# Output stores and 25 of the 35 intermediate stores issued from ScalarE instead of SyncE, in a fused attention and SoLU feed-forward kernel

## The chip, the cores and the metric

The kernel runs on one core of a Trainium2 chip. The metric is device microseconds from the start of the program to its end, the median of several executions. The engines named below are TensorE (PE in the profile, with PEld for its weight loads), VectorE (DVE), ScalarE (ACT), GpSimd (POOL) and SyncE (SP), which in this kernel does nothing but issue DMAs. "SPq" is SyncE's instruction queue. An engine executes its instructions strictly in the order in which they were written; engines wait for each other and for DMAs on semaphores.

## The reference

```python
# q, k, v: batch 8, heads 8, sequence S = 576, head size 64
out_d   = softmax(q_d @ k_d.T / 8) @ v_d       # q, k, v averaged over groups of 4 rows
out_up  = repeat(out_d, 4)                      # back to 576 rows
scores  = where(|i - j| < 4, q @ k.T / 8, -1e9)
x       = out_up + softmax(scores) @ v          # (8*576 = 4608 tokens) x 512
h       = x @ w_in                              # 4608 x 1024
solu    = h * softmax(h)
ln      = (solu - mean) / sqrt(var + 1e-6) * g_ln
y       = ln @ w_out                            # 4608 x 512, float32
```

## The kernel before

The work is cut in two ways. The attention half runs over batches and, in them, over head pairs and windows of the sequence: DMAs bring in pieces of q, k and v (tiles `qm`, `km`, `vw`, `vs`), VectorE and TensorE transpose them (`qT`, `kT`, `plT`, `pdT`), TensorE forms scores (`sc`, `sd`) and products with v (`xp`, `po`), ScalarE takes exponentials (`pl`, `pd`) and copies results out of PSUM. It ends in tiles `x` of 128 channels by tokens. The feed-forward half runs over 36 tiles of 128 tokens. All large products are done with float32 split into a high and a low part (`xh`, `xl`; `wi_h`, `wi_l`; `uh`, `ul`; `wo_h`, `wo_l`), three matmuls in place of one.

A feed-forward tile `i` goes through four generators:

- `ffn_in(i)`: 24 matmuls `h` (L862), the negated row maximum `nmx` on VectorE (L870), `e = exp(h - max)` on ScalarE (L874), `e = h * e` on VectorE (L877), two small operations on GpSimd, and then `e = e + nmu`, the centred value that is called `u`: on ScalarE (L900) or on VectorE (L902), as a table of step numbers says (`engine(...)`). Then `u` is stored to a DRAM buffer (L910, 512 KB), and after it come `r` (L913), `va`, and `m2` (L919), a Square on ScalarE that overwrites `e` and so waits until the store has read it.
- `ffn_back(i)`: four DMAs bring `u` back from DRAM with rows and columns arranged for a block transpose (tile `v`, L942). They wait until `u`'s store has landed.
- `ffn_ut(i)`: VectorE transposes `v` in place (L963), ScalarE rounds it to `uh` (L970), GpSimd or VectorE forms `ul` (L973).
- `ffn_out(i)`: 24 matmuls `o` (L990), ScalarE scales them out of PSUM into `osb` (L997, two buffers), and the tile of the output is stored (L999, 256 KB).

Tile 35 alone transposes on TensorE and has no store of `u`.

Nothing is reordered by a scheduler. Each `yield` ends a step; the steps are numbered (`plan`), and a table `ORDER` of those numbers, written out in the file, says in which order they are recorded. Every engine gets its own instructions in that order. All DMAs of the kernel before are issued by SyncE, which works through them one by one.

Each DMA reports its landing on one of eight semaphores, DMAHW0 to DMAHW7. They are handed out in turn, in the order in which the DMAs of the whole program were recorded, whichever engine issues them. The instruction that issues a DMA waits until the DMA that had the same semaphore before it has reported.

Of the kernel before, what the change touches and what calls it, by code (L numbers as in the profile page):

```python
# [122 lines left out]
"""  # L123


OTHER = """
# [11 lines left out]
def pooled_local_attention_then_solu_ffn(  # L138
# [11 lines left out]
    P = 128  # L150
# [705 lines left out]
    def ffn_in(i):  # L856
# [41 lines left out]
        else:  # L898
            if engine(nc.scalar, nc.vector) is nc.scalar:
                nc.scalar.activation(e, e, AF.Identity, bias=nmu, scale=1.0)  # L900
            else:
                nc.vector.tensor_scalar(  # L902
                    out=e, in0=e, scalar1=1.0, scalar2=nmu, op0=ALU.mult, op1=ALU.add
                )
# [255 lines left out]
```

## Time and profile before

| | |
|---|---|
| time, median of 3 runs | 583.42 us (582.59 to 588.86) |
| span of the profiled execution | 587.5 us |
| PE busy | 568.1 us (97% of the span) |
| DVE, ACT, POOL busy | 472.5, 333.4, 298.9 us |
| DMAs issued by SP | 668, of which 35 store `u` and 36 store the output |

For the profiled execution only its span is given, 587.5 us; it lies 4.1 us above the median and inside the range of the runs. Busy time is the sum of the stretches in which an engine executes. A row of the timeline has the start and the duration in us, the engine, the line, the operation, `out<-in` by the names of the program, and in square brackets how long the engine had idled and for whom. A row of the windows has, for one stretch of time, the busy us of PE, PEld, DVE, ACT and POOL (each with its count of instructions), then the granted clock of TensorE (1.00 is full speed), the busy share of the DMA engines and GB/s.

### The profile page before, as it was taken

To read this page: it belongs to the slowest core of one execution; us is meant where nothing else is said; L and a number is where in the kernel's file an instruction comes from. 1 tells how busy PE (TensorE), PEld (TensorE's weight loads), DVE (VectorE), ACT (ScalarE), POOL (GpSimd) and SP (SyncE) were. 2 spreads that over 40 slices of the span, in tenths; PEclk is the share of its full clock that TensorE was granted. 3 is DMA by queue.
4 is the path that set the end of the run, shared out by engine and by line. 5 is a ranking of instruction groups with operands and counts; after the bars stand their busy time and mean duration, and the time that the engine had idled before them with its cause. 6 is when DMAs were issued, how large, how long until landed. Compare 5 with 4: busy or idle time off the path is not lost.

```text
span 587.5 us, 15257 instructions
## 1 busy us (share of the span) xinstructions
PE 568.1 (97%) x5852; PEld 437.2 (74%) x5852; DVE 472.5 (80%) x779; ACT 333.4 (57%) x750; POOL 298.9 (51%) x447
## 2 busy tenths in 40 slices
PE   7899989999999997999999999999999999999997
PEld 3676667777777775877777777777777777788875
DVE  7999999899898878897988876898879777644650
ACT  4788678468546644466475653457545664453452
POOL 3767588857373744358543455357431842433130
PEclk9999999999999996999999999999999999999999
DMA  8999767788877888577867887665666245314221
GB/s 279 288 218 229 169 140 183 196 183 172 220 160 183 187 197 181 154 167 180 180 152 198 222 197 192 155 192 152 177 190 133 91 142 164 113 44 167 89 91 54
DMA packets 207113, 99.59 MB, mean 170 GB/s; under 512 B 163136, under 2 KB 193344, under 8 KB 207040
## 3 DMA queue, kind: packets, MB, share of 16 engines
q1 hardware_dynamic: 207040, 98.61, 65.7%
q8 instruction: 46, 0.75, 0.6%
q14 instruction: 27, 0.22, 0.1%
HBM read 65.54 MB, written 27.79 MB: 159 GB/s over the span
## 4 chain that ended last, share of the span: by engine, by line
PE 72%; DVE 13%; DMA 4%; POOL 4%; ACT 3%; issue 2%; SPq 0%; DVEq 0%; ACTq 0%; POOLq 0%
PE o L990 30%; PE h L862 28%; PE po L844 2%; PE sc L695 2%; PE sd L788 2%; DMA v<-u 2%; PE xp L753 2%; PE pdt L823 2%; PE sc L607 1%; DVE nmx L870 1%; DVE w L375 1%; DVE e L877 1%; DMA vs<-in_v_dram 1%; PE plt L655 1%; DVE w L379 1%
## 5 line engine op out<-in xcount | busy, mean ns | idle before, releaser
L862 PE MATMUL h<-wi_h,xh 128*128 128x512 f32 x288 | 116.9, 406 | 1.4 <-DVE e L877 1.3
L990 PE MATMUL o<-wo_h,uh 128*128 128x512 f32 x288 | 117.4, 408 | 0.4 <-ACT osb L997 0.4
L862 PE MATMUL h<-wi_h,xl 128*128 128x512 f32 x288 | 114.4, 397 | 0.7 <-POOL xl L1024 0.7
L990 PE MATMUL o<-wo_l,uh 128*128 128x512 f32 x288 | 114.6, 398 | 0.0
L862 PE MATMUL h<-wi_l,xh 128*128 128x512 f32 x288 | 113.7, 395 | 0.0
L990 PE MATMUL o<-wo_h,ul 128*128 128x512 f32 x288 | 79.0, 396 | 0.0
L973 POOL TENSOR_TENSOR ul<-v,uh 128x512 fp32r<-128x512 f32 x40 | 51.8, 1296 | 43.6 <-ACT uh L970 35.5
L874 ACT ACTIVATE e<-h,nmx 128x1024 f32<-128x1024 f32 x36 | 40.1, 1114 | 47.1 <-DVE nmx L870 43.4
L862 PEld LDWEIGHTS h<-wi_h,xh 128*128 128x128 f32 x288 | 54.1, 188 | 16.7 <-issue 2.9
L990 PEld LDWEIGHTS o<-wo_h,uh 128*128 128x128 f32 x288 | 54.6, 189 | 15.8 <-issue 1.4
L862 PEld LDWEIGHTS h<-wi_h,xl 128*128 128x128 f32 x288 | 54.1, 188 | 15.3 <-POOL xl L1024 2.1
L990 PEld LDWEIGHTS o<-wo_h,ul 128*128 128x128 f32 x288 | 54.1, 188 | 13.4 <-DVE ul L973 0.3
L990 PEld LDWEIGHTS o<-wo_l,uh 128*128 128x128 f32 x288 | 54.7, 190 | 12.2
L870 DVE TENSOR_REDUCE nmx<-h 128x1 f32<-128x1024 f32 x36 | 43.7, 1215 | 24.8 <-PE h L862 24.8
L862 PEld LDWEIGHTS h<-wi_l,xh 128*128 128x128 f32 x288 | 54.1, 188 | 12.0
L877 DVE SCALAR_TENSOR_TENSOR e<-h,e 128x1024 f32<-128x1024 f32 x36 | 43.8, 1216 | 14.8 <-ACT e L874 14.7
L970 ACT ACTIVATE uh<-v 128x512 fp32r<-128x512 f32 x70 | 42.7, 624 | 20.7 <-issue 8.5
L963 DVE STREAM_TRANSPOSE v<-v 128x512 f32<-128x512 f32 x70 | 46.4, 688 | 4.2 <-DMA v<-u 4.1
L997 ACT ACTIVATE osb<-o,s 128x512 f32<-128x512 f32 x36 | 24.5, 681 | 40.4 <-PE o L990 24.8
L1024 POOL TENSOR_TENSOR xl<-x,xh 128x512 fp32r<-128x512 f32 (+1 forms) x26 | 32.6, 1256 | 22.3 <-ACT xh L1021 22.0
L487 POOL TENSOR_TENSOR vs<-vs 72x512 f32<-72x512 f32 x24 | 31.6, 1318 | 17.0 <-DMA vs<-in_v_dram 16.7
L882 POOL TENSOR_SCALAR nmu<-su 128x1 f32<-128x1 f32 x36 | 8.2, 228 | 59.8 <-DVE e L877 56.9
(128 smaller groups left out, 1124.0 us busy)
## 6 DMA issues: line engine op xcount, KB each, us to landing
u<-e SPq DMA_DIRECT2D x35, 512.0 KB
v<-u SPq DMA_DIRECT2D x140, 128.0 KB
vs<-in_v_dram SPq DMA_DIRECT2D x32, 288.0 KB
out_dram<-osb SPq DMA_DIRECT2D x36, 256.0 KB
qm<-in_q_dram SPq DMA_DIRECT2D x96, 72.0 KB
km<-in_k_dram SPq DMA_DIRECT2D x96, 72.0 KB
vw<-in_v_dram SPq DMA_DIRECT2D x80, 64.0 KB
vw<-in_v_dram SPq DMA_DIRECT2D x40, 128.0 KB
```

Of the source, the lines that this page charges most:

```text
L487: eng.tensor_tensor(out=vs[:, :, 0:2 * D], in0=vs[:, :, 0:2 * D], in1=vs[:, :, 2 * D:4 * D], op=ALU.add)
L695: nc.tensor.matmul(at[rows(wi), par, pr], bt.qT[rows(par), pr, s0:s0 + W], bt.kT[rows(par), pr, s0:s0 + W], start=True, stop=True,)
L862: nc.tensor.matmul(hps[:, n, :], src[:, cc, :], wt[:, cc, n * 512:(n + 1) * 512], start=(cc == 0 and src is xh and wt is wi_h), stop=(cc = ...
L870: nc.vector.tensor_reduce(out=nmx, in_=hf, op=ALU.max, axis=AX.X, negate=True)
L874: nc.scalar.activation(e, hf, AF.Exp, bias=nmx, scale=1.0, accum_out=se)
L877: nc.vector.scalar_tensor_tensor(out=e, in0=hf, scalar=1.0, in1=e, op0=ALU.mult, op1=ALU.mult, accum_out=su)
L963: nc.vector.transpose(vg, vg)
L970: nc.scalar.activation(uh, tp, AF.Copy)
L973: (usual if v is None else engine(usual, nc.vector)).tensor_tensor(out=ul, in0=tp, in1=uh.bitcast(F32), op=ALU.subtract)
L990: nc.tensor.matmul(o, src[:, j, :], wt[:, 4 * g + j, :], start=(g == 0 and j == 0 and src is uh and wt is wo_h), stop=(g == 1 and j == 3 a ...
L997: nc.scalar.activation(osb, o, AF.Copy, scale=s)
L1024: engine(nc.gpsimd, nc.vector).tensor_tensor(out=l, in0=src, in1=h.bitcast(F32), op=ALU.subtract)
```

## The change

All 36 stores of the output are issued by ScalarE. The store of `u` is issued by the engine that `issuer` names: ScalarE where ScalarE made `u` (25 tiles), SyncE where VectorE did (10 tiles). In `ORDER`, the step of each such store is moved right behind the step that produces its data; all other steps keep their order. (The lines after L900 stand two lines lower afterwards: L912 is the store of `u`, L999 `osb`, L1001 the store of the output.)

```diff
@@ ffn_in
-            if engine(nc.scalar, nc.vector) is nc.scalar:
+            issuer = engine(nc.scalar, nc.vector)
+            if issuer is nc.scalar:
                 nc.scalar.activation(e, e, AF.Identity, bias=nmu, scale=1.0)
             else:
+                issuer = nc.sync
                 nc.vector.tensor_scalar(
                     out=e, in0=e, scalar1=1.0, scalar2=nmu, op0=ALU.mult, op1=ALU.add
                 )
...
             away[i] = dram.tile([P, DFF], F32, tag="u", name=f"u_{i}")
-            nc.sync.dma_start(away[i], e)
+            issuer.dma_start(away[i], e)
@@ ffn_out
-        nc.sync.dma_start(out[i * P:(i + 1) * P, :], osb)
+        nc.scalar.dma_start(out[i * P:(i + 1) * P, :], osb)
@@ ORDER (two of its lines; 312 and 337 are steps of stores that moved up)
-492 677 678 701 323 702 668 679 425 427 324 325 310 311 517 348 680 349 713 328 329 330 331 332
+492 677 678 701 323 702 668 679 425 427 324 325 310 311 312 517 348 680 349 713 328 329 330 331
+332 652 518 519 326 511 512 367 333 681 520 714 682 334 335 521 368 369 676 352 688 336 337 725
```

SyncE issues 607 DMAs afterwards in place of 668, ScalarE 61 in place of none. The order on TensorE, VectorE and GpSimd is the same as before.

**Place A, ScalarE, around `u` of tile 4 and the output of tile 2.** `e_4` is the tile from which `u_4` is stored, `osb_2` the output tile 2; `plT`, `mxd`, `pd` belong to the attention of batch 2, `uh_3_0` to the feed-forward of tile 3. In square brackets stand the semaphores that an instruction waits for. Before:

```order
L900 ACTIVATE e_4_2206<-e_4_2206,nmu_4_2218 128x1024 [waits Pool_49]
L636 ACTIVATE pl_1_108<-pl_1_108 128x4x128
L997 ACTIVATE osb_2_2233<-o_2_2114,s_2_1782 128x512 [waits DMAHW3_49]
L263 ACTIVATE plT_2_1_2279<-plt_2_1_2209 128x512 [waits PE_49]
L799 ACTIVATE mxd_2_1_2227<-mxd_2_1_2227 128x3 [waits DVE_49]
```

and now:

```order
L901 ACTIVATE e_4_2207<-e_4_2207,nmu_4_2219 128x1024 [waits Pool_49]
L912 DMA u_4_2228<-e_4_2207 128x1024 [waits DMAHW3_49,Activation_49]
L636 ACTIVATE pl_1_108<-pl_1_108 128x4x128
L999 ACTIVATE osb_2_2236<-o_2_2115,s_2_1782 128x512 [waits DMAHW2_49]
L1001 DMA out_0_dram<-osb_2_2236 128x512 [waits DMAHW7_49,Activation_49]
L263 ACTIVATE plT_2_1_2281<-plt_2_1_2210 128x512 [waits PE_49]
L799 ACTIVATE mxd_2_1_2230<-mxd_2_1_2230 128x3 [waits DVE_49]
```

Two DMAs have come in between the activations, each with a wait on a semaphore of the eight.

**The same place on SyncE.** `qm_3` and `km_3` are the loads of q and k of batch 3, in groups of four. Before:

```order
L910 DMA u_4_2275<-e_4_2206 128x1024 [waits DMAHW5_49,Activation_49]
L286 DMA qm_3_2051<-in_q_dram 32x18x32 [waits DMAHW6_49]
L286 DMA qm_3_2051<-in_q_dram 32x18x32 [waits DMAHW7_49]
L286 DMA qm_3_2051<-in_q_dram 32x18x32 [waits DMAHW0_49]
L286 DMA qm_3_2051<-in_q_dram 32x18x32 [waits DMAHW1_49]
L286 DMA km_3_2052<-in_k_dram 32x18x32 [waits DMAHW2_49]
```

and now the rows down to the load of `v_4`:

```order
L286 DMA km_3_2056<-in_k_dram 32x18x32 [waits DMAHW2_49]
L286 DMA km_3_2056<-in_k_dram 32x18x32 [waits DMAHW3_49]
L286 DMA km_3_2056<-in_k_dram 32x18x32 [waits DMAHW4_49]
L286 DMA km_3_2056<-in_k_dram 32x18x32 [waits DMAHW5_49]
L286 DMA qm_3_2055<-in_q_dram 32x18x32 [waits DMAHW6_49]
L286 DMA qm_3_2055<-in_q_dram 32x18x32 [waits DMAHW7_49]
L286 DMA qm_3_2055<-in_q_dram 32x18x32 [waits DMAHW0_49]
L286 DMA qm_3_2055<-in_q_dram 32x18x32 [waits DMAHW1_49]
L286 DMA km_3_2056<-in_k_dram 32x18x32 [waits DMAHW2_49]
L286 DMA km_3_2056<-in_k_dram 32x18x32 [waits DMAHW4_49]
L286 DMA km_3_2056<-in_k_dram 32x18x32 [waits DMAHW5_49]
L286 DMA km_3_2056<-in_k_dram 32x18x32 [waits DMAHW6_49]
```

The stores of `u_4` and of output tile 2 are gone from SyncE. In the last four rows DMAHW3 is passed over, since ScalarE's store of `u_4` has it, and DMAHW7 is passed over behind them, since ScalarE's store of the output has it. So the store of `u_4` waits for the second row shown here (a `km_3`), and the store of the output for the sixth (a `qm_3`), both issued by SyncE.

**Place B, ScalarE, around `u` of tile 7 and the output of tile 5**, now (before, the two DMA rows are absent):

```order
L901 ACTIVATE e_7_2872<-e_7_2872,nmu_7_2938 128x1024 [waits Pool_49]
L912 DMA u_7_2946<-e_7_2872 128x1024 [waits DMAHW2_49,Activation_49]
L999 ACTIVATE osb_5_2966<-o_5_2890,s_5_2425 128x512
L1001 DMA out_0_dram<-osb_5_2966 128x512 [waits DMAHW4_49,Activation_49]
L723 ACTIVATE pl_3_2_2754<-pl_3_2_2754 128x1024 [waits Pool_49]
```

Here the store of `u_7` waits for the last of four `plT_3_0` loads (L741), and the store of the output for the second of the four `qm_4` loads that follow those on SyncE.

133 rows, old and new, of the table ORDER are left out of this document.

## The prediction

> **What bounds the kernel now.** The page's first line says which engine sets the pace.
>
> ```profile
> PE 568.1 (97%) x5852; PEld 437.2 (74%) x5852; DVE 472.5 (80%) x779; ACT 333.4 (57%) x750; POOL 298.9 (51%) x447
> ```
>
> TensorE works in all but 587.5 − 568.1 = 19.4 us. Nothing here makes its 5852 matmuls fewer or shorter, so a gain can only come from those 19.4 us, or from stretches in which its clock is low. The windows say where both are.
>
> ```profile
> 102.00:220.30 118.30, 117.14 (x1244) 90.31 (x1240) 102.05 (x170) 69.69 (x164) 71.11 (x104) 1.00 0.81 188
> 220.30:235.00 14.70, 11.06 (x166) 8.54 (x159) 12.73 (x15) 6.63 (x13) 6.25 (x10) 0.65 0.87 181
> 235.00:540.00 305.00, 304.36 (x2814) 238.88 (x2813) 243.51 (x393) 162.32 (x368) 144.14 (x235) 1.00 0.60 159
> ```
>
> From 102 us to 540 us TensorE misses 1.16 + 3.64 + 0.64 us, so there is one gap that counts, behind 220.3 us, and the clock of that stretch is 0.65. The rest of the 19.4 us lies before 102 us and behind 540 us, where the first loads and the last tile are waited for. The timeline of TensorE has the gap, the windows of one us each its clock.
>
> ```profile
> 221.50 0.53 PE L823 MATMUL pdt<-ident,pd 64*72 64x64 f32 x12 [0.75 <-POOL pd L812]
> 226.03 1.13 PE L695 MATMUL sc<-kT,qT 64*64 64x64 f32 x32 [2.90 <-DVE pdT L265]
> 226.00:227.00 1.00, 0.97 (x32) 0.94 (x32) 0.64 (x1) 0.00 (x0) 0.00 (x0) 0.50 0.73 118
> 233.00:234.00 1.00, 1.00 (x4) 0.71 (x4) 1.00 (x2) 0.18 (x1) 0.87 (x1) 0.50 0.89 148
> 234.00:235.00 1.00, 1.00 (x5) 0.82 (x4) 0.33 (x2) 0.35 (x1) 0.38 (x2) 0.71 0.79 128
> 235.00:236.00 1.00, 1.00 (x20) 0.59 (x22) 0.00 (x0) 1.00 (x2) 0.00 (x0) 1.00 0.16 18
> ```
>
> 0.75 + 2.90 = 3.65 us of idling; then eight windows at half speed and one at 0.71, which cost 8 × 0.50 + 0.29 = 4.3 us. The chain that ended last says what the gap waits for:
>
> ```profile
> 210.49 6.49 DMA v<-u
> 217.11 1.31 DVE v L963 x2
> 218.41 1.59 DVE vs L487
> 220.03 3.79 DVE vd L490
> ```
>
> a load of `v` that SyncE issued at 210.5, late by its own queue: between 150 and 212 us it waits for almost nothing.
>
> ```profile
> SPq L286 <- DVE ul L973: 0.7, 1, 0.7
> SPq L741 <- DMA vs<-in_v_dram: 0.6, 1, 0.6
> ```
>
> SyncE is the bound of the loads there, and stores cost its queue time: the median is the second of three numbers (ns).
>
> ```profile
> L910 SPq DMA_DIRECT2D u<-e x35: 326/397/1798, 70.5 to 559.2; - x35
> L999 SPq DMA_DIRECT2D out_dram<-osb x36: 333/430/1274, 120.8 to 584.4; - x36
> ```
>
> **The change, part by part.** (1) SyncE loses 25 × 0.397 + 36 × 0.430 = 25.4 us of issuing, about a third of it before 235 us. That is worth at most the gap and its slow clock, since TensorE is dense elsewhere: −3.6 and −4.3 us. The Trainium skill, "DMA: Bandwidth & Descriptors", section "Issuing engines are not separate DMA queues", says that DMAs started by several engines interleave on the same 16 DMA engines and that only the sequencer's time to start them is saved, usually little. By that alone the sum would be between 580 and 584; the rows agree on the size of what is saved, and this rule has no cost in it.
>
> (2) ScalarE gets 61 issues. The trace has none on ScalarE; the nearest rows are SyncE's, 0.40 and 0.43 us, together about 25 us, on an engine busy 333.4 of 587.5 us. Most fall into its idle time. Reading what follows each store, I find some five places where TensorE reads ScalarE's next result with less slack than that. From nothing to 5 × 0.43 = 2.2 us; I take **+1**.
>
> (3) Each of the 61 issues **waits for a DMA of SyncE**, and ScalarE's next instructions stand behind it. This is the term that decides. The eight semaphores are handed out over both queues in recorded order, so a store on ScalarE can't go before the DMA eight places ahead has landed, and SyncE is behind the recorded order for as long as it is the bound. Before, the stores stood in SyncE's own queue, where eight places ahead was long past. At place A the lag is read from SyncE's rows against ScalarE's and TensorE's:
>
> ```profile
> 120.79 1.27 SPq L999 DMA_DIRECT2D out_dram<-osb  x1
> 122.11 2.55 SPq L286 DMA_DIRECT2D qm<-in_q_dram  x4
> 132.21 0.34 SPq L910 DMA_DIRECT2D u<-e  x1
> 135.76 3.92 SPq L286 DMA_DIRECT2D km<-in_k_dram  x4
> 139.72 2.12 SPq L286 DMA_DIRECT2D qm<-in_q_dram  x4
> 130.22 1.14 ACT L900 ACTIVATE e<-e,nmu 128x1024 f32<-128x1024 f32 x1
> 131.78 0.68 ACT L997 ACTIVATE osb<-o,s 128x512 f32<-128x512 f32 x1
> 132.35 0.60 ACT L263 ACTIVATE plT<-plt 128x512 f32<-128x512 f32 x1
> 136.78 0.61 ACT L970 ACTIVATE uh<-v 128x512 fp32r<-128x512 f32 x1
> 136.30 0.69 PE L665 MATMUL xp<-plT,vw 64*64 64x58 f32 x32
> 137.82 0.48 PE L990 MATMUL o<-wo_h,uh 128*128 128x512 f32 x1
> ```
>
> `osb_2` is made at 131.78, and its store must now wait for the second `qm_3` of the group at 139.72. That is issued at 139.72 + 2.12/4 = 140.25, and lands a transfer later; the nearest small transfer in the chain is
>
> ```profile
> 204.93 2.63 DMA plT<-pl
> ```
>
> so at 142.9. From this I take what SyncE has gained until then: the stores that stood at 120.3 to 122.1 and at 132.2 give 1.81 + 0.38 = 2.2, earlier ones about 0.9 (more can't arrive, since the loads of `v` wait for the `u` stores, which are no earlier), together 3.1. ScalarE goes on at 142.9 − 3.1 + 0.4 for the issue = 140.2, where before it went on at 132.35. TensorE needs `plT` at 136.30 and gets it at 140.8: 4.5 us late. It then needs `uh_3_0`, behind 3.7 us of ScalarE's work: 140.2 + 3.7 + 0.6 = 144.5, where `o` stood at 137.82: **6.7 us late**. TensorE has nothing to put in between, its order being fixed.
>
> At place B it is the same again.
>
> ```profile
> 190.74 2.24 SPq L286 DMA_DIRECT2D qm<-in_q_dram  x4
> 178.33 1.06 ACT L723 ACTIVATE pl<-pl 128x1024 f32<-128x1024 f32 x1
> 184.88 1.24 ACT L970 ACTIVATE uh<-v 128x512 fp32r<-128x512 f32 x2 [1.73 <-DVE v L963]
> ```
>
> The store of output tile 5 waits for the second `qm_4`: 190.74 + 0.56 + 2.63 = 193.9, less what SyncE has gained. With no gain ScalarE resumes at 194.3, with 5 us (3.1 from A, two more stores here and those between) at 189.3. I take 192, near the middle, because the engines are by then 6.7 us late and SyncE has to wait for them in places where it did not. `uh_6_0` follows 2.0 us of work later, or about 194.1 in place of 184.88: TensorE, which had no slack there, stands **9.2 us late in all** (11.5 with no gain; 6.7, A's alone, with 5).
>
> Behind B SyncE has caught up, the loads lead, and the gap at 221 to 226 us is filled: −3.6 and −4.3. The Trainium skill, "DMA: Bandwidth & Descriptors", section "Anatomy of one DMA", says that a wait for a semaphore is served on the sequencer that issues the DMA, before dispatch, and never in the DMA engines. No run here shows a DMA on ScalarE; served in the DMA queue instead, the stall of (3) would be nothing and the first rival would hold.
>
> (4) Until about 380 us more stores wait, by 1 to 3 us each in the same reckoning, against ScalarE's idle time; from 0 to 4 us, I take **+1.5**. Later SyncE waits for ScalarE, not the reverse,
>
> ```profile
> SPq L999 <- ACT osb L997: 41.1, 10, 7.7
> SPq L942 <- DMA u<-e: 23.8, 11, 3.8
> ```
>
> and there a store by ScalarE is free of stall. This waiting lies where TensorE is dense, so its removal brings nothing.
>
> (5) The gap at A is longer than the one at 226 that halved the clock, so I add the same price, **+4.3** (0 at the lower end; 8.6 if B does it too).
>
> **Sum**, against the profiled execution: 587.5 − 3.6 − 4.3 + 9.2 + 1.0 + 1.5 + 4.3 = 595.6, rounded to **596**. That execution lies 4.1 us above the median of 583.42, about the price of its slow stretch; the other runs may not have had that stretch. Against the median I then read the same sum as 583.4 − 3.6 + 16.0 = 595.8, so the forecast is 2.1% slower. Ends: nothing for clock and issue with 6.7 us of stall gives 587.5 − 7.9 + 6.7 + 1.5 = 588; the upper ones, 587.5 − 7.9 + 11.5 + 2.2 + 4 + 8.6, give 606.
>
> **The rivals.** *SyncE gains more than it costs ScalarE.* Freed early, SyncE would keep ahead, the DMAs eight places ahead would have landed, and the gap and its clock go: 587.5 − 7.9 = 580, or 576 with some of the idling before 102 us, above which nothing is to be had. For it speaks that SyncE waits for nothing from 150 to 212 us; against it that at A the lag is 10 us and the gain 3. It decides against my forecast if SyncE's lead at 140 us grows by about 10 us in place of 3.1. This is the case on the other side: faster.
>
> *The stalls are absorbed.* ScalarE is idle for 43% of the span; if it, VectorE and GpSimd run ahead at A and B by more than the rows show, 3 to 5 us of stall reach TensorE, and the gap pays for them: 587.5 − 7.9 + 4 + 1 + 1.5 = 586; 581 to 589. Against it stand the two readers without slack, `xp` and `o`.
>
> *It does not do what it says:* if ScalarE's stores had semaphores of their own, part (3) would be nothing. The program's waits name the shared eight, so I give this no chance apart from the first rival's.
>
> **How the numbers follow.** The forecast has 0.69 (588 to 606), the first rival 0.13 (576 to 581), the second 0.18 (581 to 589). A measurement of this kernel tells about 1% from no change, 577.6 to 589.3. Faster than that is a part of the first rival, 0.09; slower is the forecast less a little at its low end, 0.68; the rest, 0.23, is within. The range leaves out the best half of the first rival and the last of the forecast's tail: 580 to 607.
>
> **What would show it.** In the profile after: ScalarE rows behind a store with idle time put down to a DMA, at A about 7 to 8 us and at B a further one; TensorE gaps before `xp` near 137 us and before `o`, some 4 to 7 us together, with a clock of 0.5 behind them; no gap and no slow clock where `sc` waited for `pdT`; SyncE's total of waits larger from 150 us on. The forecast is wrong if TensorE stays dense from 102 to 220 us: then either SyncE was faster than 3.1 us ahead, or the wait is not where I put it. It is too low if `v` loads get later than at present, since the stalled ScalarE delays the stores of `u` on which they wait.

## The result, and the profile after

The changed kernel takes **607.19 us** (median; 606.28 to 608.75), the kernel before 586.14 us in the same comparison: a ratio of 1.038, 95% interval 1.031 to 1.044. It is slower, as forecast; 607.2 lies just above the range that was given (580 to 607), and the loss is nearly twice the one forecast (2.1%).

The profiled span is 605.3 us; that execution took 607.1 us, 1.8 us more than its span. The kernel before, with a span of 587.5, was thus profiled in an execution of about 589.3 us, one of the upper ones of its range (582.59 to 589.27).

The page of the changed kernel: busy time, the chain that ended last, and the new queue.

```profile
PE 569.4 (94%) x5852; PEld 437.7 (72%) x5852; DVE 468.6 (77%) x779; ACT 336.4 (56%) x750; POOL 298.1 (49%) x447
PE 61%; SPq 13%; DVE 8%; DMA 7%; ACT 4%; issue 4%; POOL 2%; ACTq 0%; DVEq 0%; POOLq 0%
q10 hardware_dynamic: 8784, 22.55, 9.7%
```

TensorE does the same 5852 matmuls and idles 605.3 − 569.4 = 35.9 us in place of 19.4. SyncE's queue, off the chain before, is now 13% of it. The windows say where the idling lies (PE busy is the second number, its granted clock the third from the end).

```profile
102.00:220.30 118.30, 104.37 (x1076) 80.20 (x1073) 90.00 (x154) 64.20 (x149) 63.59 (x97) 0.97 0.69 166
232.26:245.52 13.26, 13.26 (x263) 10.11 (x265) 10.13 (x16) 4.73 (x10) 4.24 (x6) 1.00 0.70 147
245.00:250.80 5.80, 0.93 (x34) 0.56 (x32) 0.45 (x2) 2.94 (x6) 0.81 (x1) 0.88 0.93 211
203.00:205.00 2.00, 2.00 (x6) 1.52 (x6) 2.00 (x4) 1.94 (x10) 1.44 (x2) 0.50 0.13 46
252.00:256.00 4.00, 4.00 (x54) 3.34 (x55) 3.75 (x5) 3.56 (x5) 0.19 (x1) 0.50 0.80 232
```

13.9 us are missing between 102 and 220 us, where before it was 1.16, and 4.9 just ahead of 250.8. The old gap is gone: the matmuls on both sides of it, now at 232 to 245 us, run without a break and at full clock. Two stretches at half clock follow the two long gaps. The gaps of TensorE over 0.5 us between 100 and 260 us, in its timeline (one of 0.64 us at 145.4, behind ScalarE, is left out):

```profile
106.32 1.29 PE L607 MATMUL sc<-kT,qT 64*64 64x64 f32 x64 [1.35 <-DVE pdT L265]
113.67 0.51 PE L992 MATMUL o<-wo_h,uh 128*128 128x512 f32 x1 [1.33 <-ACT uh L972]
124.03 0.50 PE L862 MATMUL h<-wi_h,xh 128*128 128x512 f32 x1 [1.73 <-ACT xh L1023]
144.11 0.69 PE L665 MATMUL xp<-plT,vw 64*64 64x58 f32 x32 [0.58 <-ACT plT L263]
147.75 0.50 PE L992 MATMUL o<-wo_h,uh 128*128 128x512 f32 x1 [1.02 <-ACT uh L972]
199.89 1.23 PE L844 MATMUL po<-pdT,vd 72*64 72x144 f32 x8 [6.62 <-ACT pdT L263]
250.80 1.14 PE L695 MATMUL sc<-kT,qT 64*64 64x64 f32 x32 [4.87 <-ACT pdT L263]
```

All but the first wait for ScalarE; the first waits for VectorE. ScalarE's timeline shows what it waited for ("ACTq" is ScalarE's queue issuing a DMA; the idle time is printed at the next activation):

```profile
122.87 0.34 ACTq L1001 DMA_DIRECT2D out_dram<-osb  x1
123.26 0.72 ACT L1023 ACTIVATE xh<-x 128x256 fp32r<-128x256 f32 x2 [2.94 <-DMA qm<-in_q_dram]
193.24 0.33 ACTq L912 DMA_DIRECT2D u<-e  x1
193.62 0.69 ACT L999 ACTIVATE osb<-o,s 128x512 f32<-128x512 f32 x1 [6.91 <-DMA plT<-pl]
194.62 0.38 ACTq L1001 DMA_DIRECT2D out_dram<-osb  x1
247.35 0.33 ACTq L912 DMA_DIRECT2D u<-e  x1
247.78 0.41 ACT L263 ACTIVATE pdT<-pdt 72x288 f32<-72x288 f32 x1 [6.68 <-DMA vw<-in_v_dram]
```

`osb` does not read `plT`, and `pdT` does not read `vw`. What stood ahead of them on ScalarE were the stores of `u_7` and of `u_10`, each waiting for the SyncE DMA that had its semaphore before. SyncE's row for the first:

```profile
188.03 3.65 SPq L741 DMA_DIRECT2D plT<-pl  x4
```

The last of these four was issued at 189.92, and the store went out at 193.24, 3.3 us later. `u_7` had been ready since 186.71. So the wait stands on ScalarE's own queue and holds its next activation back until 193.62. The Trainium skill, "DMA: Bandwidth & Descriptors", section "Anatomy of one DMA", says that any wait for a semaphore happens on the issuing sequencer, before dispatch. The trace agrees, with these 6.5 us on ScalarE.

Since each engine's order is unchanged, the start of one and the same matmul can be compared in both traces. How late TensorE is, by stretch:

| matmul at (before) | at (after) | late | what lies between |
|---|---|---|---|
| 100.01 | 101.84 | +1.8 | 0.9 of it in the first 60 us |
| 105.91 | 109.05 | +3.1 | gap 1.35 behind VectorE's `pdT` |
| 125.18 | 132.34 | +7.2 | stores of output tiles 0 and 1 |
| 137.82 (`o`, place A) | 147.75 | +9.9 | stores of `u_4` and output tile 2 |
| 180.13 | 189.15 | +9.0 | nothing |
| 187.07 (behind place B) | 204.93 | +17.9 | store of `u_7`: gap 6.6, half clock 2.2 |
| 215.22 | 232.26 | +17.0 | nothing |
| 236.03 (behind the old gap) | 245.52 | +9.5 | the old gap and its half clock are gone |
| 245.00 | 262.00 | +17.0 | store of `u_10`: gap 4.9, half clock 2.7 |
| 583.09 | 600.97 | +17.9 | |

### The profile page after: what moved, and what is told of

It is laid out like the page before. It is cut to its first block, busy times and chain, and to the rows that moved or that the text cites. A ratio compares the mean times of both kernels' runs of the same rounds, so it can differ in the third digit from the quotient of the medians.

```text
span 605.3 us, 15235 instructions
## 1 busy us (share of the span) xinstructions
PE 569.4 (94%) x5852; PEld 437.7 (72%) x5852; DVE 468.6 (77%) x779; ACT 336.4 (56%) x750; POOL 298.1 (49%) x447
## 4 chain that ended last, share of the span: by engine, by line
PE 61%; SPq 13%; DVE 8%; DMA 7%; ACT 4%; issue 4%; POOL 2%; ACTq 0%; DVEq 0%; POOLq 0%
PE o L992 25%; PE h L862 24%; SPq L286 7%; SPq L741 2%; DMA vw<-in_v_dram 2%; PE sd L788 2%; PE po L844 2%; PE xp L753 2%; DMA qm<-in_q_dram 1%; SPq L944 1%; PE pdt L823 1%; SPq L305 1%; PE sc L607 1%; PE sc L695 1%; DMA vs<-in_v_dram 1%
## 5 line engine op out<-in xcount | busy, mean ns | idle before, releaser
L999 ACT ACTIVATE osb<-o,s 128x512 f32<-128x512 f32 x36 | 24.6, 682 | 42.9 <-PE o L992 25.0
L921 ACT ACTIVATE e<-e 128x1024 f32<-128x1024 f32 x35 | 36.7, 1048 | 1.7 <-ACT osb L999 0.9
```

The source lines that it names most:

```text
L921: nc.scalar.activation(e0, e, AF.Square, accum_out=m2)
L999: nc.scalar.activation(osb, o, AF.Copy, scale=s)
```

## The experiments

In all of them the ten stores of `u` that VectorE made stay on SyncE, and a store that is not named stands as in the kernel before. Ratios are to the kernel before, with 95% intervals.

**Only the order.** The changed `ORDER`, all stores issued by SyncE.

```diff
-            issuer.dma_start(away[i], e)
+            nc.sync.dma_start(away[i], e)
-        nc.scalar.dma_start(out[i * P:(i + 1) * P, :], osb)
+        nc.sync.dma_start(out[i * P:(i + 1) * P, :], osb)
```

> All stores stay on SyncE, but in the changed order (each of the 61 stores right behind the step that produces its data). Theory 1 (a store on ScalarE waits for the SyncE DMA that had its semaphore before, so ScalarE stalls): no wait for a DMA of the rotation on ScalarE, so none of the gaps at 114, 124, 148, 200 and 251 us of the changed kernel; SyncE waits for the data of the stores instead, 583 to 592 us. Rival (the place of the stores, not the engine, costs the time): about 607 us.

Measured: 643.37 us, 1.096 (1.089 to 1.104). Neither theory had this. SyncE's waits:

```profile
SPq L991 <- ACT osb L989: 117.2, 21, 16.0
```

117.2 us where it was 41.1. A store right behind its producer, in SyncE's one queue, holds all loads behind it until the data are there. ScalarE as the issuer takes that wait away and so loses less than the new order alone would on SyncE; the late places of the old order were what kept the stores out of the loads' way.

**The early 20, and the late 41.** Stores of `u` of tiles 0 to 10 and of output tiles 0 to 8 on ScalarE; then, in another kernel, all the others.

```diff
+U_AWAY = (0, 1, 2, 3, 4, 5, 6, 7, 8, 9, 10)      # the other kernel: the 14 from 11 on
+OUT_AWAY = (0, 1, 2, 3, 4, 5, 6, 7, 8)           # the other kernel: 9 to 35
-            nc.sync.dma_start(away[i], e)
+            (nc.scalar if i in U_AWAY else nc.sync).dma_start(away[i], e)
-        nc.sync.dma_start(out[i * P:(i + 1) * P, :], osb)
+        (nc.scalar if i in OUT_AWAY else nc.sync).dma_start(out[i * P:(i + 1) * P, :], osb)
```

> Only the stores of u of tiles 0 to 10 and of the output of tiles 0 to 8 (20 of 61) are moved to ScalarE; the rest stands as before. Theory 1: these are the ones for which SyncE is behind, so nearly the whole loss is there, 602 to 608 us. Rival (each issue costs ScalarE time, 61 alike): a third of the loss, about 592 us.

> The other 41: u from tile 11 and the output from tile 9 on are moved to ScalarE, the early 20 stand as before. Theory 1: the waits are 3.5 us at most and lie beside idle time of ScalarE, 583 to 588 us, and the gap before TensorE's sc at 226 us stays. Rival (issue cost): two thirds of the loss, about 600 us.

Measured: 607.04 us, 1.034 (1.027 to 1.041), and 589.64 us, 1.005 (0.9995 to 1.010). The loss is in the early 20. The other 41 issues cost at most a per cent, and nothing that can be told from zero; the old gap stays:

```profile
225.94 1.13 PE L687 MATMUL sc<-kT,qT 64*64 64x64 f32 x32 [2.58 <-DVE pdT L257]
```

So the number of issues on ScalarE is not the cause. The early 20 came out as expected; the late 41 lie 1.6 us above the range of theory 1 and far from the rival's 600.

**The same 61 from GpSimd.** In the built program GpSimd's DMAs turn on eight other semaphores.

```diff
-            issuer.dma_start(away[i], e)
+            (nc.gpsimd if i in U_AWAY else nc.sync).dma_start(away[i], e)
-        nc.scalar.dma_start(out[i * P:(i + 1) * P, :], osb)
+        nc.gpsimd.dma_start(out[i * P:(i + 1) * P, :], osb)
```

> The 61 stores in the changed order, issued by GpSimd, whose DMAs have eight semaphores of their own in the built program. Theory 1: no wait for SyncE's DMAs; GpSimd waits for ScalarE's data at each of them and pays for the issue, but it is idle for half the span: 578 to 592 us, without the gaps of 6.6 and 4.9 us before po and sc. Rival (taking the stores from SyncE, or their place, is what costs): 600 us or more.

Measured: 613.39 us, 1.044 (1.037 to 1.051); theory 1 failed, and the time is one that the rival had. The two gaps behind ScalarE's stalls are gone, but others stand behind GpSimd, which waits for the data of the stores as SyncE did in the first run:

```profile
POOL out_dram L991 <- ACT osb L989: 61.9, 19, 11.5
```

This run does not isolate the semaphores, since it puts another wait in their place.

**The wait without a store.** 20 DMAs of 512 bytes on ScalarE at the places of the early stores; all stores stay on SyncE.

```diff
+                if i in U_TINY:
+                    nc.scalar.dma_start(dram.tile([1, P], F32, tag=f"tu_{i}", name=f"tu_{i}", bufs=1), ident[0:1, :])
...
+        if i in OUT_TINY:
+            nc.scalar.dma_start(dram.tile([1, P], F32, tag=f"to_{i}", name=f"to_{i}", bufs=1), ident[0:1, :])
```

> The kernel before, all its stores on SyncE in their old places; added are 20 DMAs of 512 bytes on ScalarE, from a constant to a buffer that nothing reads, at the places where the change puts the early stores (u of tiles 0 to 10, output of tiles 0 to 8). No data of the kernel is moved or awaited by them: only the issue and the wait for the semaphore of the rotation are added. Theory 1 (this wait is the cost): 603 to 620 us, with gaps of TensorE behind ScalarE at the same operations as in the changed kernel. Rival (the stores themselves cost by where they stand, or 20 issues of 0.35 us do): 583 to 592 us.

Measured: 591.81 us, 1.013 (1.009 to 1.017): less than the theory said, and inside the rival's range. ScalarE does wait for loads that none of its operands need,

```profile
176.44 0.63 ACT L975 ACTIVATE uh<-v 128x512 fp32r<-128x512 f32 x1 [4.30 <-DMA qm<-in_q_dram]
```

but with 20 more DMAs in the rotation each turn falls to another DMA. At place B, ScalarE's two small DMAs follow `qm` loads issued at 183.49 and 184.16, and not the `plT` load behind them. The run shows that the wait comes without any store; how long it is depends on which DMA the turn falls to, so the run does not decide by its time between the theory and the rival.

**Three stores given back, and 14.** The first without `u_7`, `u_10` and output tile 5, the second without all 14 whose SyncE DMA was late by over 4 us between 105 and 245 us.

```diff
-U_AWAY = (0, 1, 2, 3, 4, 5, 6, 7, 8, 9, 10, 11, ...)
+U_AWAY = (0, 1, 2, 3, 4, 5, 6, 8, 9, 11, ...)       # with 14 given back: (0, 1, 2, 9, 11, ...)
-OUT_AWAY = (0, 1, 2, 3, 4, 5, 6, 7, 8, 9, ...)
+OUT_AWAY = (0, 1, 2, 3, 4, 6, 7, 8, 9, ...)         # with 14 given back: (6, 7, 9, ...)
```

> The changed kernel with three stores given back to SyncE at their old places: u of tiles 7 and 10 and the output of tile 5, behind which the two long gaps stand (6.6 us before po at 200 us, 4.9 us before sc at 251 us). Theory 1: both gaps and the half clock behind them go, 6.6 + 2.2 + 4.9 + 2.7 = 16 us, if SyncE does not fall back: 590 to 597 us, the rest being the stalls at 113 to 148 us. Rival (the loss belongs to the whole set): a twentieth of it goes, 605 us.

> The changed kernel with all 14 stores given back to SyncE whose SyncE DMA of the rotation landed over 4 us after the data were ready in the trace of before, between 105 and 245 us (u of tiles 3 to 8 and 10, output of tiles 0 to 5 and 8); 47 stay on ScalarE. Theory 1: as before, 582 to 588 us, and no gap behind ScalarE over 1.5 us. Rival (issue cost): 47 of 61 parts of the loss, about 601 us.

Measured: 593.53 us, 1.016 (1.011 to 1.021), and 588.17 us, 1.006 (1.002 to 1.010). Both agree with theory 1, the second at the very end of its range. Three stores of 61 carry more than half of the loss, and with 14 given back little is left. In the second run's profile the old gap is gone too, with 47 stores on ScalarE:

```profile
220.30:235.00 14.70, 14.70 (x300) 11.41 (x299) 13.69 (x20) 8.83 (x16) 7.36 (x11) 1.00 0.80 184
```

The span is 583.3 us, but that execution (585.09 us) lies 3.1 us below this kernel's median, and SyncE issued the load of `v` behind the gap no earlier than before (210.28 us against 209.02). So the run does not show that moving these 47 closes the gap. The median is no better than that of the kernel before: no version tried here beats it.

**Only the output, only u, and each with the other's place held by a small DMA.**

The code is that of the runs above, with these sets (the first two have no small DMAs):

```diff
+U_AWAY, OUT_AWAY = (), range(36)                                # output only
+U_AWAY, OUT_AWAY = (0, 1, ... 30, 34), ()                       # u only, all 25
+U_AWAY, OUT_AWAY, U_TINY, OUT_TINY = range(11), (), (), range(9)    # u and small DMAs
+U_AWAY, OUT_AWAY, U_TINY, OUT_TINY = (), range(9), range(11), ()    # output and small DMAs
```

> Only the 36 output stores are moved to ScalarE; all stores of u stay on SyncE at their old places. Theory 1: the DMAs eight places ahead change, with 5 of 36 behind by 4 us or more in the trace of before (output tiles 0, 3, 4, 5, 8; 7.4 us at most): 588 to 600 us. Rival (it is the u stores that cost, since the loads of v wait for them): 583 to 587 us.

> Only the 25 stores of u that ScalarE made are moved to ScalarE; the output stores stay on SyncE at their old places. Theory 1a (a ring: ScalarE waits for SyncE's DMA, the store of u is held back by that, and SyncE's load of v waits for the store): with the output stores alone 12 us of the changed kernel's 21 to 24 us were there, so 592 to 600 us, with waits of SyncE for u near 14 us before 260 us. Rival 1b (the output stores and the u stores only add waits on ScalarE, nothing comes back from SyncE): 587 to 592 us.

> The 11 early stores of u are moved to ScalarE, and ScalarE issues a DMA of 512 bytes without use at the 9 places of the early output stores, which themselves stay on SyncE. So ScalarE has its 20 waits as in the run with small DMAs alone (591.8 us), and only u's data go by them. Theory 1a: the ring is closed, 598 to 607 us. Rival 1b: 590 to 594 us, the waits being the same.

> The counterpart: the 9 early output stores are moved to ScalarE, small DMAs without use stand at the 11 places of the early u stores, and u is stored by SyncE at the old places. Theory 1a: nothing waits for an output store, so no ring; as with the small DMAs alone, 588 to 594 us. Rival 1b: the same; rival (the output stores are what costs): 598 us or more.

Measured: output only 595.74 us, 1.022 (1.019 to 1.025); u only 605.73 us, 1.035 (1.027 to 1.043); u with small DMAs 606.13 us, 1.036 (1.028 to 1.044); output with small DMAs 596.04 us, 1.017 (1.011 to 1.024), above what theories 1a and 1b gave it and below the third. Output only is as theory 1 expected. With `u` and small DMAs the time is in the range of the ring (theory 1a), with `u` only 6 us above it. SyncE's waits for `u` before 260 us are 10.6 and 10.4 us in these two, against 1.5 in the kernel before. But the traces show another difference as well: it is another DMA that is waited for. The stall at place B with output only, with u and small DMAs, and with output and small DMAs:

```profile
189.63 1.06 ACT L715 ACTIVATE pl<-pl 128x1024 f32<-128x1024 f32 x1 [3.82 <-DMA qm<-in_q_dram]
```

```profile
192.72 0.69 ACT L994 ACTIVATE osb<-o,s 128x512 f32<-128x512 f32 x1 [9.34 <-DMA plT<-pl]
```

```profile
188.16 0.69 ACT L994 ACTIVATE osb<-o,s 128x512 f32<-128x512 f32 x1 [3.10 <-DMA qm<-in_q_dram]
```

With the stores of `u` on ScalarE, that of tile 7 gets the turn behind `plT`; where the first DMA at this place is an output store or a small DMA in another rotation, it gets the turn behind an earlier `qm`. In all five traces in which `u_7` has the turn behind `plT` (changed kernel, early 20, `u` only, `u` and small DMAs, three alone) its store went out 2.1 to 3.3 us after the last `plT` was issued. The store of output tile 5 in the output-only kernel was issued at 189.25, 2.15 us after the `qm` that it followed (187.10).

A part of the ring is in the trace of the changed kernel: behind place B, SyncE waits for GpSimd's `pl`, whose exponential stands on ScalarE right behind the stalled store of output tile 5.

```profile
SPq L741 <- POOL pl L731: 12.0, 1, 12.0
```

How much of the stall at `u_10` comes from this stays open; that `u_10` was among the late ones in the trace of before (the DMA that has its turn was issued at 229.12, its data were ready at 225.05) says that some of it is its own.

**Three stores alone.**

```diff
+U_AWAY = (7, 10)
+OUT_AWAY = (5,)
```

> The kernel before with three stores alone moved to ScalarE: u of tiles 7 and 10 and the output of tile 5. Taking these three out of the changed kernel gave back 13 to 14 us. Theory 1 (each is a wait of its own behind SyncE's queue): most of it comes with them, 592 to 600 us, with ScalarE idle for a DMA of SyncE for some 7 us or more before 200 us. Rival (they cost only because SyncE and ScalarE are already late by the stores before them): 583 to 589 us.

Measured: 603.01 us, 1.032 (1.030 to 1.034), 3 us above the range of theory 1 and far from the rival's. Three of 61 stores make most of the loss (3.2% of 3.8%), in a trace whose TensorE runs within 0.1 to 0.4 us of that of before until 184 us. SyncE's waits for `u` before 260 us are only 3.5 us here, so the ring is not needed for a loss of this size. SyncE, ScalarE and TensorE at place B:

```profile
186.80 2.47 SPq L733 DMA_DIRECT2D plT<-pl  x4
```

```profile
176.33 1.14 ACT L892 ACTIVATE e<-e,nmu 128x1024 f32<-128x1024 f32 x1
190.80 0.34 ACTq L902 DMA_DIRECT2D u<-e  x1
191.20 0.69 ACT L989 ACTIVATE osb<-o,s 128x512 f32<-128x512 f32 x1 [13.72 <-DMA plT<-pl]
192.60 1.06 ACT L715 ACTIVATE pl<-pl 128x1024 f32<-128x1024 f32 x1 [0.72 <-DMA qm<-in_q_dram]
196.99 0.41 ACT L255 ACTIVATE pdT<-pdt 72x288 f32<-72x288 f32 x1 [2.81 <-DVE pdT L257]
```

```profile
197.45 1.23 PE L836 MATMUL po<-pdT,vd 72*64 72x144 f32 x8 [13.39 <-ACT pdT L255]
```

`u_7` is ready at 177.48 and its store goes out at 190.80, 2.1 us after the fourth `plT` was issued (188.68). ScalarE idles for 13.7 us, TensorE for 13.4. The early stores in the traces of the changed kernel, of the output stores only and of these three agree: those that waited went out 2 to 6 us after the DMA that their semaphore named had been issued, whatever that DMA was; where that DMA had been out for 6 us or more, the store followed its producer by 0.03 us.

In the changed kernel the same stall is 6.9 us, because TensorE is 9 us late there already: SyncE's queue reaches its `plT` at about the same time (186.8 and 188.0), so what the stores ahead cost is not added to it. That is why the early stalls, the 14 given back and the three alone don't add up: 593.5 without the three, 603.0 with nothing but them, 607.2 with all.

## Why the prediction was off, step by step

Against the profiled execution the forecast was +8.1 us, and the measured loss is 17.8 = 15.7 + 2.2 − 7.6 + 7.5. The 9.7 between them are +6.5 in the delay behind place B (term 3: 15.7 in place of 9.2), +6.0 at `u_10`, its half clock included (term 4: 7.5 in place of 1.5), −2.1 in the half clock (term 5: 2.2 at B in place of 4.3 at A), −1.0 in the issues (term 2, counted as nothing here) and +0.3 in the old gap. So two steps failed, what follows B and the size of (4).

- **The bound: right. The price of the old gap: right, but not its reason.** The old gap and its half clock were put at −7.9; measured from 215 to 236 us, 17.0 to 9.5, it is −7.6. Term (1) gave this to SyncE, which loses 61 stores. SyncE did not get ahead by that: at A its second `qm_3` was issued at 139.21, 1.0 us earlier than before and not 3.1; at B its second `qm_4` at 192.36, 1.0 later than before, where the forecast had counted on some 2.3 earlier. The load of `v` that the gap waited for was issued 11.2 us later than before (210.49):

```profile
221.72 3.91 DMA v<-u
```

  TensorE was 17.0 us late by then, so the load was in time because the rest came later. The load is also not the whole of the gap. VectorE idled 2.15 us for it; then `vd`, a row that the prediction shows and did not read, took 3.79 us, and in the changed kernel it takes a ninth of that:

```profile
233.94 0.42 DVE L490 TENSOR_TENSOR vd<-vs 72x256 f32<-72x256 f32 x1
```

  In the five traces in which this `vd` takes 3.8 us (before, late 41, GpSimd, small DMAs, three given back) a gap of 1.0 to 2.9 us stands before `sc`, in two of them although VectorE hardly waits for `v` (0.03 us). In the other nine it takes 0.4 to 1.5 us, and there is no gap before `sc`. In the five GpSimd is busy all through `vd`, and wherever `vd` takes 0.42 us GpSimd stands idle beside it; whether that is the reason was not tested. That the size came out right is therefore luck.
- **The mechanism of (3): right**, and place B was put within 3 us: ScalarE was to go on at 192, and goes on at 195.04, with the three alone at 192.60.
- **The step that failed in (3)** is what follows B. It let `uh_6_0` be the first thing that TensorE reads, 2.0 us behind. The first is `po`, which stands at 184.19 in the trace of before and waits for `pdT`, and that stands behind `pl` on ScalarE, VectorE's work and 2.8 us more of waiting, a row that the trace of before has and the prediction did not read:

```profile
182.74 0.41 ACT L263 ACTIVATE pdT<-pdt 72x288 f32<-72x288 f32 x1 [2.83 <-DVE pdT L265]
```

  `po` came at 199.89, so TensorE was 15.7 us late there and not 9.2: 3.0 from ScalarE's later start, since SyncE had gained nothing, and 3.5 from the chain behind it.
- **(4) was mis-sized.** It gave +1.5 to all stores but A's and B's. Before A TensorE loses 5.3 us (1.8 to 7.2 late): 1.3 behind VectorE's `pdT` (a gap of 0.9 to 1.4 us that stands in the six traces with the first stores of `u` on ScalarE and in no other; how it comes about was not followed) and 4.0 at the stores of output tiles 0 and 1. These do not add to B, for the reason above. The store of `u_10` does: it brings back 7.5 us (9.5 to 17.0), as much as the vanished gap gave. In the trace of before the DMA that has its turn was issued 4.1 us after its data were ready; I took ScalarE's idle time behind it for cover, and the idling lay behind `pdT`, which TensorE needs.
- **Place A: less than half of what was said.** 2.8 us in place of 6.7, since TensorE and ScalarE arrived there some 7 to 9 us late (output tile 2 ready at 141.12 in place of 132.46) and SyncE 1.0 us early. ScalarE's waits there are 1.0 and 1.9 us.
- **(5), the half clock at A: absent.** The gaps there are 0.58, 0.64 and 1.02 us, not one of 4 to 7; the half clock came at B (2.2 us) and at `u_10` (2.7).
- **(2): right in that it is small.** The issues on ScalarE cost nothing that can be told from zero (1.005, interval 0.9995 to 1.010, with 41 of them). The Trainium skill, "DMA: Bandwidth & Descriptors", section "Issuing engines are not separate DMA queues", says that only the sequencer's time to start a DMA is saved by issuing from several engines. The runs agree that little is saved, and show besides that a second issuing engine can lose far more than that by its wait, 3.8% here.
- **The sign at the end came true.** The prediction called itself too low if the loads of `v` get later: SyncE waits 53.2 us for `u` in all, against 23.8.
- **The semaphores.** That they are handed out in the order of recording, as the description of the kernel has it, is not exact. Between engines the built program has an order of its own: the store of `u_4` takes its turn in the middle of a load step that was recorded after it, and `u_7` its turn behind the `plT` loads of place B, recorded after it too, as the numbers of the instructions in the built program show. By recording, `u_7` would have stood behind a `qm_4` that SyncE issued at 180.41 in the run of three alone, in place of the `plT` at 188.68; no run tried that order. The prediction read the pairs from the built program, so its pairs are right.
- **The median.** The prediction put the profiled execution 4.1 us above the median; that compares its span with the others' times, and by time it lies about 589.3 − 583.4 = 5.9 above. Taking the gap's 3.6 us off the median as well supposed that the median has the gap. Eleven executions of the kernel before in the later comparisons, of 581.7 to 584.7 us, have a mean granted clock of 1.000, so they had no stretch at half clock to win back. Against the profile the loss is 605.3 − 587.5 = 17.8 us, against the median 21.

## What to carry to other kernels

Before a DMA is moved to another engine's queue, read in the built program which DMA it has to wait for (the order in which the DMAs were written does not tell), and whether the engine that issues that one runs late; a compute engine that is ahead of the loading queue is tied to it by a single such DMA (three stores cost 3.2%). Such a stall is priced by when the other queue arrives, not by how much is queued, so several of them overlap and taking one away shows the next. After a stall, follow the stalled engine's own next instructions through to the first one that TensorE reads, over the other engines too.

## What the runs showed that was not expected

A store placed right behind its producer in the queue that also does all the loads cost 9.6% (643 us): SyncE waited 117 us for `osb`, against 41 at the late places.

TensorE's clock fell to half behind gaps of 4.9, 6.6 and 13.4 us, but among the shorter gaps the length alone does not tell. Behind gaps of 2.57 us (stores from GpSimd, at 134 us) and 2.09 us (only the order, at 161 us) it stayed at 1.00; behind 2.40 us (GpSimd, at 150 us) and 2.04 us (small DMAs, at 231 us) it fell to 0.50. With three stores given back, two gaps of 1.10 and 1.15 us with 1.0 us of work between them were enough:

```profile
110.00:112.00 2.00, 2.00 (x6) 1.52 (x6) 2.00 (x6) 0.00 (x0) 0.58 (x2) 0.50 0.03 10
```

In the changed kernel a single gap of 1.73 us left the clock at 1.00.
